# Nine pairs' probabilities transposed as float32r, mean and 1/sigma spread by transposes, PSUM banks taken one by one

## The chip, the core and the metric

One Trainium2 chip, one of its cores. The metric is device time in microseconds (us), from the program's first to its last instruction on that core; lower is better. The kernel before takes 863.33 us (median of 3 runs, 862.97 to 863.5).

## The reference

Causal attention over 4 batches, 12 heads, 448 positions and a head size of 64, in float32, and behind it a layer norm and a feed-forward block with 768 -> 3072 -> 768 and a residual:

```python
scores = scale * np.matmul(q, k.transpose(0, 1, 3, 2))
scores = np.where(mask, -1000000000.0, scores)          # causal
attn = np.exp(scores - np.max(scores, axis=-1, keepdims=True))
attn = attn / (np.sum(attn, axis=-1, keepdims=True) + 1e-09)
x = np.matmul(attn, v)                                  # heads side by side: (4, 448, 768)
xn = (x - mu) / np.sqrt(var + 1e-06) * g_ln
out = x + np.maximum(xn @ w_ch1, 0.0) @ w_ch2
```

## The kernel before

Everything is kept to float32 accuracy. A matmul of float32 operands goes through TensorE in two recorded passes; most matmuls therefore take operands that are split into two float32r parts (high and low, such as wh and wl, xh and xl, kh and kl) and run as three (or two) single-pass float32r matmuls that add up in PSUM.

The work is cut by batch. Two heads make a pair: six pairs for each batch, 24 in all. The 448 positions are cut into four blocks of 112. For a pair, `scores` (or `both`, in batch 0) makes the causal scores in PSUM tiles `sc`; `least` masks, scales and finds the row minimum on VectorE into the SBUF tile `P`; `exps` takes the exponential on ScalarE; `norm` scales P's rows by 1/sum (on GpSimd, VectorE or ScalarE; in the trace `P<-P,r`); `transposes` turns the ten 112x112 blocks of each head with TensorE (`pt<-ident,P`, five groups of four a pair) and moves each group to SBUF as `PT`; `pv` multiplies by the values (`px<-PT,vt`, in batch 0 `px<-PT,rest`) into one PSUM tile in which one head has the upper and the other the lower 64 partitions. Behind the six pairs, `stats` transposes the result for mean and variance (`pln`), `aggr` makes mean and 1/sigma per position, and `spread` (for the last two batches `Pair.banks`) writes them across all 128 partitions (`mb`, `rb`) by multiplying a column, broadcast to 128 columns, with the identity.

The feed-forward block of batches 0 and 1 is `ffn`: 96 steps of 36 matmuls of 448 columns (`ph` into the hidden layer, `po` out of it), with three PSUM banks in rotation (tag `mm`). Weights are converted and split during batch 0 and written to device memory (`keep`, `keep_parts`); later they are read back (`load_full`, six steps ahead; `load_parts`). Batches 2 and 3 are done together by `Pair`, in which seven matmul products take the place of eight (`bX`, `bA`, `bY`, `bZ`); its inputs are made by `inputs` (`xg`, `t` and their parts). The attention of batch 1 runs inside the feed-forward block of batch 0, that of batches 2 and 3 inside that of batch 1 and the end of that of batch 0. So a few transposes, scores or px matmuls always stand between long rows of ph and po.

Nothing is issued as it is written. Each call is recorded as a task in `Plan`; `schedule` gives each task a due time (from its place in the steps of the feed-forward block), and `run` sets the order of all five queues with a list of prices (`cost`): each engine takes the most urgent task that is ready. `together` welds matmuls into one task, so that nothing comes between them. `pick` lets VectorE, ScalarE and GpSimd wait in two cases: where GpSimd or VectorE holds their shared port, and where in the last pass a more urgent task became ready a little later. All DMAs go through SP's queue, in order; a DMA that waits for its data holds up those behind it. `reuse_waits="tile"` pools wait tile by tile; the other pools are closed and opened as a whole (`turn`): `conv` to `late`, `ap` to `pair_x`, and, when the feed-forward block of batch 1 is done, the PSUM pool `ps` to `psb`, whose eight banks `Pair` uses.

All work is issued through one line of `issue` (L513 in the trace), so the rows are told apart by the names of tiles.

Of the kernel before, what the change touches and what calls it, by code (L numbers as in the profile page):

```python
# [28 lines left out]
NF = DFF // P  # L29
HF = NF // 2  # L30
# [14 lines left out]
PASSES, PORT, LEAST, AFTER, URGENT = 6, 300, 150, 1500, 5000  # L45
# [11 lines left out]
KEEP0 = 36  # L57
IDLE = [3, 12]
# [4 lines left out]
ELAG = [2, 5, 7]  # L63
NDVE = 7
# [3 lines left out]
OFF = [C * (i * (i + 1) // 2) for i in range(NC + 1)]  # L68
# [99 lines left out]
class Plan:  # L168
# [99 lines left out]
    def cost(self, t):  # L268
# [189 lines left out]
    def pick(self, e, at, heap, start, port, need, hint, drift):  # L458
# [3 lines left out]
        while heap:  # L462
# [59 lines left out]
def kernel(ctx, tc, qk, v, w1, w2, g, out):  # L522
# [21 lines left out]
    def turn(old, new):  # L544
        def f():
            stacks[old.name].close()
            open_pool(new)

        plan.change(f, [old], [new])

    ident = const.tile([P, P], F32, name="ident")
# [98 lines left out]
    def open_late(_):  # L650
        turn(conv, late[0])
# [43 lines left out]
    class Att:  # L695
# [146 lines left out]

        def transposes(self, p, grp, eng):
# [3 lines left out]
            for h, j in grp:  # L847
# [10 lines left out]
        def pv(self, p):  # L858
# [5 lines left out]
            if self.b == 3:  # L864
                self.xT.append(late[0].tile([P, S], F32, tag="xT", name="xT", bufs=6))
            else:
                self.xT.append(sb.tile([P, S], F32, tag="xT", name="xT", bufs=12))
            for j in range(NC):
                for h in range(2):
                    nc.tensor.matmul(  # L870
                        px[D * h:D * h + D, C * j:], lhsT=vt[:, h, j, :],
                        rhs=self.t.pop(("PT", p, h, j)), start=(j == 0), stop=(j == NC - 1),
                    )
# [26 lines left out]
        def spread(self):  # L900
# [3 lines left out]
            for x in range(NC):  # L904
                nc.tensor.matmul(
                    mb[:, x * C:(x + 1) * C], lhsT=mv[:, x, 0:1].to_broadcast([C, P]),
                    rhs=ident[:C, :C], start=True, stop=True,
# [3 lines left out]
            for x in range(NC):  # L911
                nc.tensor.matmul(
                    rb[:, x * C:(x + 1) * C], lhsT=ve[:, x:x + 1].to_broadcast([C, P]),
                    rhs=ident[:C, :C], start=True, stop=True,
# [39 lines left out]
        def steps(self):  # L954
# [13 lines left out]
            for p, t0 in enumerate(t0s):  # L968
# [81 lines left out]
    class Pair:  # L1050
# [3 lines left out]
        def __init__(self, a, b):  # L1054
            self.at = a, b

# [411 lines left out]
```

## Time and profile before

| | us |
|---|---|
| median of 3 runs (lowest, highest) | 863.33 (862.97, 863.5) |
| the profiled execution, its own time | 865.12 |
| its span, first to last instruction | 863.3 |
| TensorE matmuls busy (share of the span), instructions | 850.3 (98%), 4663 |
| TensorE weight loads busy | 742.7 (86%) |
| VectorE busy | 684.2 (79%) |
| ScalarE busy | 504.4 (58%) |
| GpSimd busy | 268.4 (31%) |

The profile is of one execution. "Busy" is the time in which an engine has at least one instruction under way. Matmuls overlap: each is recorded from its start to a modelled end, so the recorded length of one (0.26 us for a transpose, 0.37 us for 448 columns) is longer than the distance to the next, and it is the distances of starts that tell what one costs. The weight loads (PEld) run ahead of the matmuls. A row of the timeline merges equal instructions in a row: x4 is four of them, and its length is from the first start to the last end.

### The profile page before, as it was taken

What the parts mean: (1) busy time and instruction counts of PE and PEld (TensorE: products, weight loads), DVE (VectorE), ACT (ScalarE), POOL (GpSimd) and SP (SyncE); (2) the same over time, 40 slices, a digit from 0 to 9 for tenths busy, and PEclk for the clock granted to TensorE, in tenths of its full rate; (3) what the DMA queues carried; (4) which work ended last, traced back from release to release, by engine and by line L of the source; (5) the groups of instructions that cost most, each with busy time, mean ns of one, the idle gap of its engine ahead of it and who ended that gap; (6) DMA issues with size and microseconds to landing.
All of it is one profiled execution on the core that took longest, in us unless ns stands there. A gap on an engine that the chain in (4) does not pass through costs nothing.

```text
span 863.3 us, 13819 instructions
## 1 busy us (share of the span) xinstructions
PE 850.3 (98%) x4663; PEld 742.7 (86%) x4663; DVE 684.2 (79%) x1454; ACT 504.4 (58%) x1111; POOL 268.4 (31%) x268
## 2 busy tenths in 40 slices
PE   8999999999999999999999999999999999999997
PEld 5579888888888888888888898989999999999997
DVE  5889888888989986777776579596887778778785
ACT  6898987788887865564454134353544435354450
POOL 4630002210023510010000038454535454464450
PEclk9999999999999999999999999999999999999999
DMA  9665786847669767765554436225243332423424
GB/s 240 222 219 215 307 327 261 320 163 291 249 252 330 261 220 243 257 213 189 186 179 143 160 132 202 93 84 159 63 136 113 93 126 79 127 90 107 123 86 144
DMA packets 59015, 159.77 MB, mean 185 GB/s; under 512 B 6720, under 2 KB 25536, under 8 KB 58944
## 3 DMA queue, kind: packets, MB, share of 16 engines
q1 hardware_dynamic: 58944, 158.89, 54.1%
q8 instruction: 37, 0.61, 0.3%
q14 instruction: 34, 0.28, 0.1%
HBM read 119.15 MB, written 39.71 MB: 184 GB/s over the span
## 4 chain that ended last, share of the span: by engine, by line
PE 89%; DVE 8%; ACT 1%; issue 1%; DMA 1%; POOL 0%; DVEq 0%; ACTq 0%
PE ph L513 21%; PE bX L513 19%; PE po L513 16%; PE bY L513 10%; PE sc L513 6%; PE px L513 6%; PE pt L513 5%; PE bA L513 5%; DVE xg L513 1%; PE pln L513 1%; DVE t L513 1%; DVE qs L513 1%; DVE P L513 1%; DVE xT L513 1%; DVE hx L513 1%
## 5 line engine op out<-in xcount | busy, mean ns | idle before, releaser
L513 ACT ACTIVATE P<-P,nm 112x448 f32<-112x448 f32 (+3 forms) x176 | 91.1, 520 | 39.7 <-DVE nm L513 39.3
L513 POOL TENSOR_TENSOR kl<-qkraw,kh 128x896 fp32r<-128x896 f32 x18 | 40.8, 2266 | 232.4 <-ACT kh L513 104.0
L513 PE MATMUL ph<-xh,wh 128*128 128x448 f32 x288 | 111.4, 388 | 0.1
L513 PE MATMUL po<-hh,wh 128*128 128x448 f32 x288 | 109.3, 383 | 1.9 <-ACT xT2h L513 1.9
L513 PE MATMUL ph<-xl,wh 128*128 128x448 f32 x288 | 105.6, 367 | 0.0
L513 PE MATMUL ph<-xh,wl 128*128 128x448 f32 x288 | 105.5, 366 | 0.0
L513 PE MATMUL po<-hl,wh 128*128 128x448 f32 x288 | 104.2, 367 | 0.0
L513 PE MATMUL po<-hh,wl 128*128 128x448 f32 x288 | 103.3, 367 | 0.0
L513 ACT ACTIVATE wp<-s 128x256 fp32r<-128x256 f32 (+1 forms) x108 | 50.1, 464 | 84.1 <-PE bX L513 35.1
L513 DVE CUSTOM_DVE_ANT_0 P<-sc,mask 112x448 f32<-112x448 f32 (+3 forms) x176 | 73.0, 444 | 26.5 <-PE sc L513 25.9
L513 POOL TENSOR_TENSOR s<-u 128x256 f32<-128x256 f32 (+1 forms) x60 | 56.5, 946 | 93.3 <-DMA u<-scratch 54.3
L513 ACT ACTIVATE wk<-u 128x384 fp32r<-128x384 f32 (+1 forms) x82 | 38.2, 467 | 65.8 <-PE bX L513 47.7
L513 DVE TENSOR_TENSOR wp<-s,wp 128x256 fp32r<-128x256 f32 (+1 forms) x120 | 72.9, 613 | 2.3 <-ACT wp L513 1.9
L513 PEld LDWEIGHTS pt<-ident,P 112*112 112x112 f32 x440 | 48.9, 133 | 15.3 <-ACT PT L513 2.7
L513 PE MATMUL pt<-ident,P 112*112 112x112 f32 x440 | 60.7, 260 | 0.5 <-ACT PT L513 0.4
L513 DVE TENSOR_TENSOR xT<-xT,bX 128x448 f32<-128x448 f32 x72 | 44.5, 618 | 20.8 <-PE bX L513 20.5
L513 POOL TENSOR_TENSOR h<-b,h 128x448 fp32r<-128x448 f32 x36 | 42.2, 1173 | 58.0 <-ACT h L513 31.8
L513 PEld LDWEIGHTS po<-hh,wh 128*128 128x128 f32 x288 | 54.1, 188 | 6.6 <-ACT xT2h L513 2.2
L513 PEld LDWEIGHTS ph<-xh,wl 128*128 128x128 f32 x288 | 54.1, 188 | 4.8
L513 PEld LDWEIGHTS po<-hh,wl 128*128 128x128 f32 x288 | 54.1, 188 | 4.8
L513 PEld LDWEIGHTS ph<-xh,wh 128*128 128x128 f32 x288 | 54.1, 188 | 4.1 <-ACT xh L513 0.4
L513 PEld LDWEIGHTS ph<-xl,wh 128*128 128x128 f32 x288 | 54.5, 189 | 3.3
(163 smaller groups left out, 2165.8 us busy)
## 6 DMA issues: line engine op xcount, KB each, us to landing
raw<-w_dram SPq DMA_DIRECT2D x39, 768.0 KB, 8.1
scratch<-w SPq DMA_DIRECT2D x48, 384.0 KB, 7.0
full<-scratch SPq DMA_DIRECT2D x24, 768.0 KB, 5.4
qkraw<-qk_dram SPq DMA_DIRECT2D x18, 896.0 KB, 5.4
kept<-wl SPq DMA_DIRECT2D x30, 384.0 KB, 6.9
u<-scratch SPq DMA_DIRECT2D x24, 384.0 KB, 3.7
u<-scratch SPq DMA_DIRECT2D x36, 256.0 KB, 2.9
rawx<-w_dram SPq DMA_DIRECT2D x9, 768.0 KB, 10.0
```

What stands on the lines that cost most here:

```text
L513: getattr(getattr(nc, t.engine), method)(*args, **kw)
```

## The change

1. The probabilities of nine pairs (pairs 3 to 5 of batch 2, and all six of batch 3; table `COPIED`) are copied after `norm`, head by head, by a DMA from P into a new tile PR of type float32r (18 DMAs of 112x1120). `transposes` then turns PR with a float32r identity into float32r PSUM. The other fifteen pairs' transposes stay float32. PR lives in a new pool `probs`, two tiles, beside `late`; the pair's `tmp` tiles move to a pool `temps` that opens where `probs` closes.
2. `spread` and `Pair.banks` call `transpose` on the broadcast column where they called `matmul` with the identity: 32 float32 matmuls become 32 float32 transposes.
3. In batch 0, `pv` welds the matmuls of the two heads of a pair (`together`).
4. `Pair` takes its PSUM banks from `ps` one by one, in the order of `BANKS`; the pool `psb` and its turn are gone.
5. The planner: other prices for DMAs and for a float32r transpose; and `pick` holds an engine back only for tasks before its time 70000 (`START`).

```diff
+COPIED = [NP, NP, 3, 0]
+BANKS = [("sc", 2), ("sc", 2), ("pt", 2), ("pt", 2), ("pv", 1), ("mm", 3), ("mm", 3), ("mm", 3)]
-PASSES, PORT, LEAST, AFTER, URGENT = 6, 300, 150, 1500, 5000
+PASSES, PORT, LEAST, AFTER, URGENT, START = 6, 300, 150, 1500, 5000, 70000
...
-            return 60, (x.p[1] - x.p[0]) * n * 4, False
+            rate = 360 if x.p[1] - x.p[0] == P else 240 if x.p[1] - x.p[0] == D else 150 if n == 512 else 330
+            return 60, (x.p[1] - x.p[0]) * n * 4 * 320 / rate, False
...
-                return 0.84 * n, 220, False
+                return 0.84 * n if t.ins[0].dtype == F32 else 56, 220, False
...
-            if shared and port > at + PORT:
+            if shared and port > at + PORT and at < START:
...
-            if hint is not None:
+            if hint is not None and at < START:
...
-    late = [pool("late", 1, reuse_waits="tile")]
+    late = pool("late", 1, reuse_waits="tile")
+    probs = pool("probs", 1, reuse_waits="tile")
+    temps = pool("temps", 1, reuse_waits="tile")
...
-    psb = pool("psb", 8, space=PSUM, reuse_waits="tile")
...
-    ident = const.tile([P, P], F32, name="ident")
+    identr = const.tile([P, P], F32R, name="ident")
+    ident = identr.bitcast(F32)
...
+        def copy(self, p, h):
+
+            t = probs.tile([C, OFF[NC]], F32R, tag="PR", name="PR", bufs=2)
+            nc.sync.dma_start(out=t.bitcast(F32), in_=self.t["P", p, h])
+            self.t["PR", p, h] = t
...
-                    nc.tensor.transpose(pt[:, o:o + C], pp[:, a:a + C], ident[:C, :C])
+                    if ("PR", p, h) in self.t:
+                        pr = self.t["PR", p, h]
+                        nc.tensor.transpose(pt[:, o:o + C].bitcast(F32R), pr[:, a:a + C], identr[:C, :C])
+                    else:
+                        nc.tensor.transpose(pt[:, o:o + C], pp[:, a:a + C], ident[:C, :C])
...
+                if self.b == 0:
+                    nc.together(*calls)
+                    continue
...
             for x in range(NC):
-                nc.tensor.matmul(
-                    mb[:, x * C:(x + 1) * C], lhsT=mv[:, x, 0:1].to_broadcast([C, P]),
-                    rhs=ident[:C, :C], start=True, stop=True,
+                nc.tensor.transpose(
+                    mb[:, x * C:(x + 1) * C], mv[:, x, 0:1].to_broadcast([C, P]), ident[:C, :C]
                 )
...
                     put(pre, t0 + nat[h], self.norm, p, h)
+                    if p >= COPIED[self.b]:
+                        put(pre, t0 + nat[h], self.copy, p, h)
...
         def open_inputs(self):
+            turn(probs, temps)
             turn(ap, pair_x)
...
-                self.bank[b, name] = psb.tile([P, S], F32, tag="b", name="b" + name, bufs=8)
+                tag, bufs = BANKS[self.banked % 8]
+                self.banked += 1
+                self.bank[b, name] = ps.tile([P, S], F32, tag=tag, name="b" + name, bufs=bufs)
...
-        turn(ps, psb)
```

The order of every queue changes. Three places follow, all on TensorE.

The opening, batch 0, where the first pair's px matmuls stand among transposes (pt) and scores (sc); a row with 64x448 is one matmul of one head. Before:

```order
L513 MATMUL pt<-ident,P 112x112 x8
L513 MATMUL px<-PT,rest 64x448
L513 MATMUL pt<-ident,P 112x112 x6
L513 MATMUL px<-PT,rest 64x448
L513 MATMUL px<-PT,rest 64x336 x2
L513 MATMUL px<-PT,rest 64x224 x2
L513 MATMUL px<-PT,rest 64x112 x2
```

Now:

```order
L516 MATMUL pt<-ident,P 112x112 x8
L516 MATMUL sc<-first_qk 112x224 x2
L516 MATMUL pt<-ident,P 112x112 x6
L516 MATMUL px<-PT,rest 64x448 x2
L516 MATMUL px<-PT,rest 64x336 x2
L516 MATMUL px<-PT,rest 64x224 x2
L516 MATMUL px<-PT,rest 64x112 x2
```

The two heads' first px matmuls stood six transposes apart and are now neighbours.

Batch 2, pair 3, the first copied pair: its second and third group of transposes among po matmuls (numbers after a name tell buffers apart; P_3364 and P_3467, later PR_3600 and PR_3680, are its two heads). Before:

```order
L513 MATMUL pt_3685<-ident_82,P_3364 112x112 [waits PE_49]
L513 MATMUL pt_3685<-ident_82,P_3364 112x112 x3
L513 MATMUL po_3584<-hh_1002,wh_3613 128x448
L513 MATMUL po_3584<-hl_1011,wh_3613 128x448
L513 MATMUL po_3584<-hh_1002,wl_3637 128x448
L513 MATMUL pt_3695<-ident_82,P_3364 112x112 [waits DVE_49]
L513 MATMUL pt_3695<-ident_82,P_3364 112x112
L513 MATMUL pt_3695<-ident_82,P_3467 112x112 x2
```

Now:

```order
L516 MATMUL pt_3707<-ident_82,PR_3600 112x112 [waits PE_49]
L516 MATMUL pt_3707<-ident_82,PR_3600 112x112 x3
L516 MATMUL po_3609<-hh_1013,wh_3483 128x448
L516 MATMUL po_3609<-hl_1023,wh_3483 128x448
L516 MATMUL po_3609<-hh_1013,wl_3520 128x448
L516 MATMUL pt_3719<-ident_82,PR_3600 112x112 [waits DVE_49]
L516 MATMUL pt_3719<-ident_82,PR_3600 112x112
L516 MATMUL po_3609<-hh_1013,wh_3483 128x448
L516 MATMUL po_3609<-hl_1023,wh_3483 128x448
L516 MATMUL po_3609<-hh_1013,wl_3520 128x448
L516 MATMUL pt_3719<-ident_82,PR_3680 112x112 [waits DMAHW2_49]
L516 MATMUL pt_3719<-ident_82,PR_3680 112x112
```

The second head's first transposes now wait for a DMA, and three po matmuls have moved ahead of them; from that pair's last scores to this place there are 71 rows in either order.

Near the end of batch 1's feed-forward block, where one po ends and the next begins. Before:

```order
L513 MATMUL po_5795<-hl_1011,wh_5765 128x448
L513 MATMUL po_5795<-hh_1002,wl_5805 128x448
L513 MATMUL po_5795<-hh_1002,wh_5765 128x448
L513 MATMUL po_5939<-hh_1002,wh_5897 128x448 [waits DVE_49,Activation_49]
L513 MATMUL po_5795<-hl_1011,wh_5765 128x448
L513 MATMUL po_5795<-hh_1002,wl_5805 128x448
L513 MATMUL po_5939<-hl_1011,wh_5897 128x448
L513 MATMUL po_5949<-hh_1002,wh_5800 128x448
```

Now:

```order
L516 MATMUL po_5903<-hh_1013,wh_5808 128x448
L516 MATMUL po_5903<-hl_1023,wh_5808 128x448
L516 MATMUL po_5903<-hh_1013,wl_5847 128x448
L516 MATMUL po_5979<-hh_1013,wh_5842 128x448 [waits DVE_49]
L516 MATMUL po_5979<-hl_1023,wh_5842 128x448
L516 MATMUL po_5979<-hh_1013,wl_5813 128x448 [waits DMAHW4_49]
```

Three banks of po were open at once (5795, 5939, 5949); now each po is finished before the next begins.

## Rows read from the trace of the kernel before

**Rows 1.** Windows: us, busy time of each engine (instructions), granted clock, DMA share, GB/s

```profile
67.00:300.00 233.00, 232.54 (x1337) 203.66 (x1336) 208.13 (x433) 191.27 (x377) 45.12 (x26) 1.00 0.73 272
300.00:505.00 205.00, 205.00 (x1214) 177.13 (x1213) 145.65 (x357) 99.33 (x244) 19.20 (x11) 1.00 0.60 200
...
550.00:859.00 309.00, 308.23 (x1509) 281.89 (x1507) 241.47 (x429) 138.56 (x304) 144.65 (x148) 1.00 0.35 110
```

**Rows 2.** The same view of two stretches of the opening (PE, PEld, DVE, ACT, POOL)

```profile
34.00:52.00 18.00, 18.00 (x128) 11.69 (x125) 14.29 (x57) 17.00 (x47) 12.29 (x24) 1.00 0.34 104
52.00:65.00 13.00, 11.96 (x79) 9.16 (x77) 12.77 (x37) 12.07 (x29) 3.13 (x2) 1.00 0.68 238
```

**Rows 3.** Timeline of TensorE: start us, us, engine, line, operation, tile, shape, count

```profile
112.60 0.55 PE L513 MATMUL pt<-ident,P 112*112 112x112 f32 x4
112.92 0.45 PE L513 MATMUL ph<-xh,wh 128*128 128x448 f32 x1
113.21 0.37 PE L513 MATMUL ph<-xl,wh 128*128 128x448 f32 x1
```

**Rows 4.** Groups of weight loads: form, count | busy us, mean ns | idle before us

```profile
L513 PEld LDWEIGHTS pt<-ident,P 112*112 112x112 f32 x440 | 48.9, 133 | 15.3 <-ACT PT L513 2.7 <-POOL P L513 2.1 <-DVE nm L513 1.4
...
L513 PEld LDWEIGHTS sc<-kl,qs 128*112 128x112 f32 x144 | 25.2, 175 | 2.4
```

**Rows 5.** Timeline of the weight loads of one group of scores

```profile
102.63 0.17 PEld L513 LDWEIGHTS sc<-kl,qs 128*112 128x112 f32 x1
102.72 0.18 PEld L513 LDWEIGHTS sc<-kh,qs 128*112 128x112 f32 x1
```

**Rows 6.** Timeline of the matmuls of the same group

```profile
102.63 0.21 PE L513 MATMUL sc<-kh,qs 128*112 128x112 f32 x1
102.68 0.26 PE L513 MATMUL sc<-kl,qs 128*112 128x112 f32 x1
```

**Rows 7.** Timeline of TensorE at batch 1's spread: its start and the stream behind it

```profile
264.75 1.04 PE L513 MATMUL mb<-ident,mv 112*128 112x112 f32 x8
...
266.74 0.36 PE L513 MATMUL po<-hl,wh 128*128 128x448 f32 x1
```

**Rows 8.** Timeline of TensorE in the opening: a split pair, and a whole one

```profile
15.88 0.96 PE L513 MATMUL px<-PT,rest 112*64 112x448 f32 x2
...
17.49 2.10 PE L513 MATMUL px<-PT,rest 112*64 112x448 f32 x14
19.52 0.79 PE L513 MATMUL pt<-ident,P 112*112 112x112 f32 x6
...
46.83 2.23 PE L513 MATMUL px<-PT,rest 112*64 112x448 f32 x16
```

**Rows 9.** Timeline of VectorE in the opening: a conversion of 128x896

```profile
24.90 0.91 DVE L513 CAST kh<-qkraw 128x896 fp32r<-128x896 f32 x1
```

**Rows 10.** Timeline of VectorE at the pair's inputs

```profile
531.24 1.55 DVE L513 TENSOR_TENSOR t<-xg,t 128x448 f32<-128x448 f32 x1
532.71 0.61 DVE L513 TENSOR_TENSOR xT<-po,xT 128x448 f32<-128x448 f32 x1
```

**Rows 11.** Timeline of TensorE there: in brackets the idle time before, and its releaser

```profile
533.47 0.45 PE L513 MATMUL po<-hh,wh 128*128 128x448 f32 x1 [1.87 <-ACT xT2h L513]
```

**Rows 12.** Timelines of ScalarE and VectorE: the last scalings of two heads

```profile
301.32 1.40 ACT L513 ACTIVATE P<-P,r 112x336 f32<-112x336 f32 x3
...
334.31 0.95 DVE L513 TENSOR_SCALAR P<-P,r 112x112 f32<-112x112 f32 x3
```

**Rows 13.** Timeline of TensorE: the groups that hold these heads' first transposes

```profile
306.59 0.55 PE L513 MATMUL pt<-ident,P 112*112 112x112 f32 x4
...
341.57 0.55 PE L513 MATMUL pt<-ident,P 112*112 112x112 f32 x4
```

**Rows 14.** DMA issues from 280 to 460 us: count, KB each, median us to landing

```profile
kept<-wl SPq DMA_DIRECT2D x20, 384.0 KB, 6.7
kept<-wl SPq DMA_DIRECT2D x9, 192.0 KB, 3.5
```

More of the change, by code (lines that the diff above doesn't have):

```diff
@@ L29 @@
 NF = DFF // P
+OFF = [C * (i * (i + 1) // 2) for i in range(NC + 1)]
 HF = NF // 2
@@ L539, with turn @@
     ap = pool("ap", 1, side="right")
-    late = [pool("late", 1, reuse_waits="tile")]
+    late = pool("late", 1, reuse_waits="tile")
+    probs = pool("probs", 1, reuse_waits="tile")
+    temps = pool("temps", 1, reuse_waits="tile")
     pair_x = pool("pair_x", 1, side="right", reuse_waits="tile")
-    psb = pool("psb", 8, space=PSUM, reuse_waits="tile")
-    def turn(old, new):
+    def turn(old, *new):
         def f():
             stacks[old.name].close()
-            open_pool(new)
-        plan.change(f, [old], [new])
-    ident = const.tile([P, P], F32, name="ident")
+            for x in new:
+                open_pool(x)
+        plan.change(f, [old], new)
+    identr = const.tile([P, P], F32R, name="ident")
+    ident = identr.bitcast(F32)
     mask = ap.tile([C, S], BF16, name="mask")
@@ L650, in open_late @@
     def open_late(_):
-        turn(conv, late[0])
+        turn(conv, late, probs)
     def weights_ahead(start):
@@ L864, in pv @@
             if self.b == 3:
-                self.xT.append(late[0].tile([P, S], F32, tag="xT", name="xT", bufs=6))
+                self.xT.append(late.tile([P, S], F32, tag="xT", name="xT", bufs=6))
             else:
@@ L868, in pv @@
             for j in range(NC):
-                for h in range(2):
-                    nc.tensor.matmul(
-                        px[D * h:D * h + D, C * j:], lhsT=vt[:, h, j, :],
-                        rhs=self.t.pop(("PT", p, h, j)), start=(j == 0), stop=(j == NC - 1),
-                    )
+                calls = [
+                    ("matmul", (px[D * h:D * h + D, C * j:],), dict(
+                        lhsT=vt[:, h, j, :], rhs=self.t.pop(("PT", p, h, j)), start=(j == 0), stop=(j == NC - 1),
+                    ))
+                    for h in range(2)
+                ]
+                if self.b == 0:
+                    nc.together(*calls)
+                    continue
+                for method, args, kw in calls:
+                    nc.tensor.matmul(*args, **kw)
             move(self.xT[p], px)
@@ L911, in spread @@
             for x in range(NC):
-                nc.tensor.matmul(
-                    rb[:, x * C:(x + 1) * C], lhsT=ve[:, x:x + 1].to_broadcast([C, P]),
-                    rhs=ident[:C, :C], start=True, stop=True,
+                nc.tensor.transpose(
+                    rb[:, x * C:(x + 1) * C], ve[:, x:x + 1].to_broadcast([C, P]), ident[:C, :C]
                 )
@@ L1062, in banks @@
                     for x in range(NC):
-                        nc.tensor.matmul(
-                            dst[:, x * C:(x + 1) * C], lhsT=col(x).to_broadcast([C, P]),
-                            rhs=ident[:C, :C], start=True, stop=True,
+                        nc.tensor.transpose(
+                            dst[:, x * C:(x + 1) * C], col(x).to_broadcast([C, P]), ident[:C, :C]
                         )
@@ L1082, in tmp @@
         def tmp(self, name):
-            return late[0].tile([P, S], F32, tag="tmp", name=name, bufs=NTMP)
+            return temps.tile([P, S], F32, tag="tmp", name=name, bufs=NTMP)
         def parts(self, src, hi, lo, eng):
@@ L1374 @@
         nc.gpsimd.affine_select(
-            out=ident, in_=ident, compare_op=ALU.not_equal, fill=1.0, base=0, pattern=[[-1, P]], channel_multiplier=1,
+            out=identr, in_=ident, compare_op=ALU.not_equal, fill=1.0, base=0, pattern=[[-1, P]], channel_multiplier=1,
         )
```

3 lines of the change are left out of this document (1 added, 2 removed).

## Prediction

> **What bounds the kernel now.** I read the stretches first. From 300 to 505 us TensorE is busy for all 205.00 us, VectorE for 145.65 and ScalarE for 99.33; from 550 to 859 us it issues 1509 matmuls in 309.00 us, which is 0.2048 us for each, and is idle for 0.8 [rows 1]. The granted clock is 1.00 in both rows, the 2.4 GHz level. So after the opening, TensorE's queue is the path: a nanosecond taken out of it there comes off the end, as long as nothing else becomes late. The opening (to about 67 us, where the dense stream of ph matmuls starts) is different: from 34 to 52 us TensorE counts as busy throughout while ScalarE is busy 17.00 of 18.00 us, and from 52 to 65 us VectorE is busy 12.77 of 13.00 [rows 2]. There three engines share the bound, and a gain of one is worth a part of itself.
>
> **Transposes of nine pairs as float32r.** Today four transposes stand in a stream of 448-column matmuls. From the start of the first to the start of the second matmul behind them is 113.21 - 112.60 = 0.61 us; less one matmul of 0.205 the four cost 0.406 [rows 3]. The four last (0.55 us from first start to last end, less the 0.26 that one of 112 columns is recorded with [rows 6]) start 0.095 apart, so 0.38 of it is their own pace and 0.026 the change from one kind to the other. What sets 0.095? Two things can: 112 columns streamed as float32, or 112 columns of weights loaded. A float32r stream of 112 columns is shown by the scores: the matmul after it starts at 102.68, 0.05 later [rows 6]. The loads are shown too: consecutive float32r loads of 112 columns start 0.09 apart (102.63, 102.72) [rows 5] and each is recorded with 175 ns [rows 4], that is some 80 to 85 ns more than its pace. A load for a transpose, of the same 112 columns, is recorded with 133 ns [rows 4]; less the same it would keep a pace of 48 to 53. So the float32 stream is today's limit, and with a float32r stream of 0.050 the load is about as long. No row shows a float32r transpose; between 0.050 (stream alone) and 0.096 (loads at the pace of the scores') I take 0.054, the upper end for a load of the short kind, since a transpose's load is of that kind already. Four then cost 4 x 0.054 + 0.026 = 0.242, a gain of 0.164. Nine pairs have five groups each: 45 x 0.164 = **7.4 us**, bounds 0 and 8.1.
>
> The Trainium skill ("TensorE: Matmul & The Clock Gate", section "LDWEIGHTS (loading the stationary operand)") gives the load as the number of columns over 1.2 per ns, whatever the data: 93 ns for 112 columns. By that rule the transposes are load-bound already and float32r gains nothing. The 0.09 us between loads of the scores agrees with it; the 133 ns recorded for a transpose's load against 175 for the same columns speaks against it.
>
> **Mean and 1/sigma by transposes.** Each spread is now eight matmuls in float32, which the trace counts as two passes each: sixteen from 264.75 until the stream is back at 266.74, less one 0.205, is 1.79 us, or 0.112 a pass [rows 7]. Eight transposes at 0.095 + 0.03 cost 0.79. There are three such spreads inside the dense stream (batch 1, and two for the pair): 3 x 1.0 = 3.0. In the opening the second half of batch 0's spread stands in front of the ph stream, 0.5 more; its first half is ready before VectorE asks. **3.5 us**, bounds 2.7 (a transpose no faster than a pass) and 4.0.
>
> **The opening.** Batch 0's probabilities times values run the two heads in two halves of the array, and side by side only if they are adjacent in the queue. Pair 0 today: 0.96 us for one head's first matmul alone, then 2.10 for the rest; a pair kept whole takes 2.23. Each has 0.07 of tail under what follows (17.49 + 2.10 = 19.59, and the next starts at 19.52), so it is 0.89 + 2.03 = 2.92 against 2.16 [rows 8]. The order shows five of six pairs split, so TensorE loses at least 5 x 0.76 = 3.8 us, and the change welds all six. But VectorE has 0.2 us of idle left from 52 to 65 us and ScalarE 1.0 from 34 to 52 [rows 2]: what TensorE finishes earlier they must also finish earlier. VectorE's idle of 3.7 us from 34 to 52 is what can be closed. I take **2.0 us**; upper bound 3.8; lower bound -0.9, because the order hands VectorE one more conversion of 128x896 ahead of the first ph, 0.91 us by its like [rows 9], and ScalarE one less.
>
> **The wait at 531 us.** TensorE stands for 1.87 us and resumes at 533.47 [rows 11]. VectorE, busy with the pair's inputs, had taken 1.55 us over one subtraction from 531.24 and only then got to the addition that empties a bank of po, from 532.71 to 533.32 [rows 10]; the first matmul of the next po waits for VectorE and ScalarE, whose own work hung on the same subtraction. Before, two po were interleaved there and ended together; in the new order they come one after the other, with some 36 matmuls (7.4 us) between the end of one and the next need of a bank. Gain **1.9**, bounds 0 and 2.3 (with the 0.46 us of idle before 300 us).
>
> **The copies.** Each of the 18 heads gets a DMA of 112x1120 float32 (490 KB) between its last scaling and its first transpose. That interval is cover only in its present length: in the order the first transpose stands as many rows behind the scores as before. The shortest, for the first copied pair: last scaling ends 301.32 + 1.40 = 302.72, and its first transpose is the third of the four from 306.59, at 306.78: 4.06 us. The pair's other head has 4.2; of the other sixteen the shortest is 334.31 + 0.95 = 335.26 to 341.57, 6.31 us [rows 12, 13], the longest 10.4, the mean 7.9. The nearest DMAs of that stretch land after 6.7 us (384 KB) and 3.5 us (192 KB) [rows 14]; both go to device memory, a copy stays on chip. I take 4.6 us: the first two heads are late by about 0.5 each, **-1.0 us**; bounds 0 (under 4 us) and -5.9 (6.7 us: 2.6 + 2.5 + 0.4 + 0.3 + 0.1). Behind a copy that waits for its scaling stand the next kept store, qkraw load and weight load (full) in SP's queue. Nobody waits soon for a kept store; the code issues full six steps ahead and qkraw four, and a step lasts 5 us (96 of them in the 482 us from 67 to 549). That cover hides a wait of a few us, and I cost it at nothing; were it gone, a late qkraw would cost TensorE the excess, which the next term's bound takes in.
>
> **Banks one by one; no look-ahead after 70 us.** None of TensorE's waits in the trace stands at the change from po to bX, where the whole PSUM pool is turned over today; so taking the banks one by one gains 0 there. The planner no longer holds VectorE, ScalarE and GpSimd back for a coming urgent task or for the shared port after its time 70000, so every order changes. TensorE's idle from 67 to 549 us is 0.46 up to 300 us, nothing to 505 [rows 1], and the 1.87 at 531, 2.3 in all; a new order can bring as much again. I take **-0.8**, bounds 0 and -2.3.
>
> Sum: 7.4 + 3.5 + 2.0 + 1.9 - 1.0 - 0.8 = **13.0 us**. The profiled execution took 865.12 us (span 863.3), so 852.1 for one like it; the median of the runs, 863.33, is 1.8 lower, and the forecast on it is **850.3 us**.
>
> **Rivals.**
> 1. Loads bind: float32r transposes keep 0.096. For it: the pace of the scores' loads [rows 5]. Against: 133 ns against 175 [rows 4]. The first term falls away: 850.3 + 7.4 = 857.7 us. By the rule of the Trainium skill above, this is what happens.
> 2. Copies land somewhat late, at 6.7 us as the kept stores do: 5.9 instead of 1.0, 855.2 us; together with other small waits up to 861.
> 3. Slower: the copies land after 9 us or more, because the DMA engines are already busy 0.60 of the time from 300 to 505 us [rows 1] and the copies add to that. Then every head waits: 4.9 + 4.8 for the first pair and 20.8 over the other sixteen (what each interval lacks of 9 us, added up), some 30 us against 14 gained: 879 us. It decides from a landing of about 7.8 us, where the sum of the waits reaches the 14. Against it: both rows of that stretch [rows 14] lie below.
> 4. The float32r matmuls do not run where they should, or new waits eat all: no change.
>
> **How the numbers follow.** Forecast (845 to 855): 0.70. Rival 1 (855 to 860): 0.15. Rival 2: 0.07. Rival 3: 0.05. Rival 4: 0.03. All best bounds give 863.3 - (8.1 + 4.0 + 3.8 + 2.3) = 845.1; the range reaches up over rival 1: 845 to 858. A measurement here tells 0.2% (1.7 us) from no change: faster 0.92, same 0.03, slower 0.05.
>
> **What would show it.** Groups of four float32r transposes in the stream costing 0.24 us instead of 0.41, and their loads still at 133 ns; spreads of eight instructions in 0.8 us; the first dense ph some 2 us earlier than 66.8; no wait at the pair's inputs; waits of TensorE on the copy for the first copied pair alone. The prediction is wrong if the transposes stay 0.095 apart, if waits on the copy come back pair after pair, or if the opening ends later than today.

## The result, and the profile after

The changed kernel takes 854.6 us (median of four) against 863.18 for the kernel before: a ratio of 0.9895, interval 0.9876 to 0.9915. In a second comparison (after_again) it took 853.83 us (853.42 to 854.09) against 864.59, ratio 0.9874, 0.986 to 0.9889. One of the first four executions, the profiled one, was disturbed (1366.73 us, at a mean granted clock of 0.656; the other three took 853.36 to 855.4) and isn't in the ratio, so every line of after below is from the second comparison's run of the same kernel, with a span of 851.9 us against 863.3.

The path is still TensorE's queue. The first view is that of the windows: stretch, busy time and instructions of PE, PEld, DVE, ACT and POOL, granted clock, DMA share, GB/s. The last window is moved by 10 us, since the pair starts at 538.95 instead of 549.19:

```profile
34.00:52.00 18.00, 15.71 (x112) 11.25 (x109) 15.30 (x47) 15.43 (x38) 11.55 (x17) 0.91 0.41 140
52.00:65.00 13.00, 10.86 (x71) 7.83 (x71) 12.63 (x35) 12.27 (x28) 3.48 (x2) 1.00 0.66 233
...
67.00:300.00 233.00, 233.00 (x1339) 203.31 (x1338) 210.48 (x432) 192.48 (x380) 45.48 (x26) 1.00 0.77 287
300.00:505.00 205.00, 205.00 (x1225) 177.59 (x1224) 153.46 (x368) 96.40 (x233) 23.97 (x15) 1.00 0.69 230
540.00:848.00 308.00, 308.00 (x1508) 281.51 (x1506) 243.43 (x432) 135.41 (x299) 144.09 (x148) 1.00 0.36 111
```

Against [rows 1], the 0.46 us of idle before 300 us is gone, and there are 11 more matmuls in the 205 us from 300 to 505. In the opening TensorE is no longer busy throughout from 34 to 52 us: 15.71 of 18.00, where [rows 2] has 18.00; and its granted clock is 0.91 there, where it was 1.00.

A group of four transposes of a copied pair, in the timeline of TensorE [rows 3]; its weight loads in their own timeline; and then all such loads from 300 to 505 us [rows 4] (count | busy us, mean ns | idle us):

```profile
363.05 0.43 PE L516 MATMUL pt<-ident,PR 112*112 112x112 f32 x4
363.32 0.45 PE L516 MATMUL ph<-xh,wh 128*128 128x448 f32 x1
363.60 0.36 PE L516 MATMUL ph<-xl,wh 128*128 128x448 f32 x1
```

```profile
362.88 0.46 PEld L516 LDWEIGHTS pt<-ident,PR 112*112 112x112 f32 x4
363.29 0.19 PEld L516 LDWEIGHTS ph<-xh,wh 128*128 128x128 f32 x1
```

```profile
L516 PEld LDWEIGHTS pt<-ident,PR 112*112 112x112 f32 x176 | 18.7, 133 | 3.9
```

From the group's start to the second matmul behind it is 0.55; less one matmul of 0.205 the four cost 0.345, where 0.406 was and 0.242 was forecast. The median of the 39 groups that stand in a clean stream is 0.342. The loads are recorded with 133 ns, as forecast. The starts of the matmuls alone would not have told it: within a group they stand 0.057 apart (median), close to the forecast's 0.054. But of the loads, the first of which runs ahead (362.88), the last starts at 363.21 (362.88 + 0.46 less 0.13) and the next one, for the ph behind, 0.08 later, and the ph starts 0.03 after its load.

A pair of px in the opening [rows 8], whole now, and batch 1's spread [rows 7], TensorE's timeline:

```profile
16.70 2.11 PE L516 MATMUL px<-PT,rest 112*64 112x448 f32 x16
...
262.94 0.55 PE L516 MATMUL mb<-ident,mv 112*128 112x112 f32 x4
263.33 0.55 PE L516 MATMUL rb<-ident,ve 112*128 112x112 f32 x4
263.64 0.46 PE L516 MATMUL po<-hh,wh 128*128 128x448 f32 x1
263.94 0.36 PE L516 MATMUL po<-hl,wh 128*128 128x448 f32 x1
```

The 16 matmuls of the pair are recorded with 2.11 in all. Eight transposes of the spread cost 263.94 - 262.94 - 0.205 = 0.79. The same reckoning gives 0.40 for the half spread in the opening (0.89 before) and 1.55 for the pair's two (3.58 before, as two of [rows 7]).

What TensorE waits for from 67 to 540 us, by groups, two of them shown (count | busy us, mean ns | idle us before):

```profile
L516 PE MATMUL pt<-ident,P 112*112 112x112 f32 x175 | 24.2, 259 | 0.0
L516 PE MATMUL pt<-ident,PR 112*112 112x112 f32 x180 | 19.4, 230 | 0.0
```

No group there has any idle time: the 1.87 us of [rows 11] are gone, and the copies are never waited for. In the DMA issues from 280 to 460 us [rows 14] the copies land sooner than the kept stores of 384 KB (count, KB each, median us to landing):

```profile
PR<-P SPq DMA_DIRECT2D x17, 490.0 KB, 4.1
kept<-wl SPq DMA_DIRECT2D x19, 384.0 KB, 6.2
kept<-wl SPq DMA_DIRECT2D x10, 192.0 KB, 3.9
```

**Where the 11.4 us between the two spans went.** Four landmarks divide a span: the start of the dense ph stream (the first ph with xl), the first bX of the pair, the last matmul, the end.

| stretch | before | after | gain |
|---|---|---|---|
| opening, to the dense stream | 66.56 | 65.11 | 1.45 |
| dense stream to the pair | 482.63 | 473.84 | 8.79 |
| the pair | 309.02 | 309.02 | 0.00 |
| last matmul to the end | 5.06 | 3.94 | 1.12 |

The middle's 8.79 are 2.6 for the float32r transposes (from the run pr_f32, below), 3.0 for the three spreads, 2.3 for the two waits that are gone, and 0.5 for five transposes that now stand ahead of the dense stream (125 instead of 120); 0.3 stays over. The last line wasn't forecast: with the end of before unchanged, the run b_weld below has 4.1 there too, so it most likely belongs to the one execution profiled of before, which is a long one (865.12 us, median 863.33), rather than to the change.

### The profile page after: what moved, and what is told of

Same layout as the page of the kernel before. It is cut to its first block, busy times and chain, and to the rows that moved or that the text cites. A ratio compares the mean times of both kernels' runs of the same rounds, so it can differ in the third digit from the quotient of the medians.

```text
span 1364.9 us, 13747 instructions
## 1 busy us (share of the span) xinstructions
PE 1355.3 (99%) x4631; PEld 882.4 (65%) x4631; DVE 696.4 (51%) x1466; ACT 508.4 (37%) x1099; POOL 265.2 (19%) x268
## 4 chain that ended last, share of the span: by engine, by line
PE 99%; DVE 0%; DMA 0%; issue 0%
PE ph L516 21%; PE po L516 21%; PE bX L516 21%; PE bY L516 11%; PE px L516 6%; PE sc L516 6%; PE bA L516 5%; PE pt L516 5%; PE pln L516 1%; PE idle L516 0%; DMA first_qk<-qk_dram 0%; PE mb L516 0%; PE rb L516 0%; DVE w L516 0%; DVE xT L516 0%; DVE stat L516 0%
## 5 line engine op out<-in xcount | busy, mean ns | idle before, releaser
L516 PE MATMUL ph<-xh,wh 128*128 128x448 f32 x288 | 157.7, 548 | 0.0
L516 PE MATMUL po<-hh,wh 128*128 128x448 f32 x288 | 155.3, 539 | 0.0
L516 PE MATMUL po<-hl,wh 128*128 128x448 f32 x288 | 152.2, 528 | 0.0
L516 PE MATMUL po<-hh,wl 128*128 128x448 f32 x288 | 152.1, 528 | 0.0
L516 PE MATMUL ph<-xl,wh 128*128 128x448 f32 x288 | 151.6, 526 | 0.0
L516 PE MATMUL ph<-xh,wl 128*128 128x448 f32 x288 | 151.5, 526 | 0.0
L516 ACT ACTIVATE wk<-u 128x256 fp32r<-128x256 f32 (+1 forms) x78 | 35.8, 461 | 156.1 <-PE bX L516 111.8
L516 PEld LDWEIGHTS ph<-xh,wh 128*128 128x128 f32 x288 | 64.3, 223 | 24.3 <-issue 9.0
L516 PEld LDWEIGHTS po<-hl,wh 128*128 128x128 f32 x288 | 64.4, 223 | 24.0 <-issue 8.5
L516 PE MATMUL bY<-h,wp 128*128 128x448 f32 x216 | 79.7, 529 | 0.0
L516 PE MATMUL bX<-h,wk 128*128 128x448 f32 x216 | 78.2, 528 | 0.0
```

The lines of the kernel that those rows point to most:

```text
L516: getattr(getattr(nc, t.engine), method)(*args, **kw)
```

## The experiments

Medians are of 4 to 11 runs, and each ratio is to runs of before on the same chip (medians 864.59 for the first five rows, 863.55 to 864.61 for the rest); load80 and stream80 ran once. "Stream" is where the dense stream starts, "idle" is TensorE's idle time from there to the pair, both in the profiled execution. load80 and stream80 leave out a part of the output.

| run | median us | ratio, interval | stream | idle | stream to pair | pair |
|---|---|---|---|---|---|---|
| before | 864.59 | 1 | 66.56 | 2.3 | 482.63 | 309.02 |
| after_again | 853.83 | 0.9874, 0.986 to 0.9889 | 65.11 | 0 | 473.84 | 309.02 |
| pr_f32 | 856.02 | 0.99, 0.9886 to 0.9915 | 64.66 | 0 | 476.48 | 308.96 |
| no_copy | 856.99 | 0.9911, 0.9897 to 0.9926 | 65.08 | 0 | 476.52 | 309.12 |
| no_weld | 857.0 | 0.9912, 0.9895 to 0.9928 | 68.01 | 0 | 474.06 | 309.26 |
| turned | 854.55 | 0.9898, 0.9885 to 0.9912 | 64.31 | 0.1 | 474.37 | 309.30 |
| load80 | 851.97 | | 65.48 | 0 | 471.75 | 308.98 |
| stream80 | 850.6 | | 64.26 | 0.2 | 471.39 | 309.10 |
| b_weld | 862.16 | 0.9986, 0.9974 to 0.9998 | 61.22 | 4.6 | 484.93 | 308.96 |
| old_prices | 857.27 | 0.9916, 0.99 to 0.9931 | 66.13 | 0 | 475.07 | 310.30 |
| hold | 863.41 | 0.9988, 0.9977 to 1.0 | 65.45 | 6.9 | 483.31 | 309.82 |
| turned_hold | 863.68 | 0.9994, 0.9985 to 1.0004 | 64.39 | 6.9 | 483.46 | 309.00 |
| cheap_copy | 858.71 | 0.9919, 0.9889 to 0.9949 | 63.40 | 7.0 | 482.30 | 309.28 |

**The changed kernel again**, as it stands.

> The changed kernel as it stands, for a profile at the full clock. Measured so far about 854 us, 4 us above the forecast of 850.3. Theory A (the transposes are mis-sized): groups of four float32r transposes cost 0.33 us or more in the stream instead of the forecast 0.24, and everything else is as forecast. Theory B (the opening gives nothing): groups at 0.24, but the dense ph stream starts no earlier than about 66.8 us. Theory C (waits on the copies): groups at 0.24, the opening 2 us shorter, and TensorE idle for 3 to 5 us in front of transposes of PR.

The lines above are its lines. Of the theories A fits: 0.345 for a group, with the stream 1.5 us earlier and no wait for PR.

**What paces a float32r transpose.** First the transposes of the copied pairs in float32 again, with the planner's price left as it was, so that TensorE's order stays:

```
-  nc.tensor.transpose(pt[:, o:o + C].bitcast(F32R), pr[:, a:a + C], identr[:C, :C])
+  nc.tensor.transpose(pt[:, o:o + C], pr[:, a:a + C].bitcast(F32), ident[:C, :C])
```

> The changed kernel with its copies, and the same order on TensorE, but the 180 transposes of copied probabilities read PR as float32 with the float32 identity. If float32r transposes keep a pace of 0.054 us, this is 7.4 us slower than the changed kernel, about 861.5. If loads bind (0.095 for either type), the same, about 854. If theory A holds, in between: about 3.5 us slower.

A group of pr_f32 in TensorE's timeline:

```profile
368.19 0.55 PE L516 MATMUL pt<-ident,PR 112*112 112x112 f32 x4
368.51 0.45 PE L516 MATMUL ph<-xl,wh 128*128 128x448 f32 x1
368.80 0.37 PE L516 MATMUL ph<-xh,wl 128*128 128x448 f32 x1
```

0.61 - 0.205 = 0.405, as in the kernel before; the stretch from the stream to the pair is 2.64 us longer than after, and the median 2.2. So the float32r transposes are worth 2.2 to 2.6 us, not 7.4. Their loads start 0.078 apart (median), where those of float32 transposes start 0.095 to 0.099 apart. Whether that 0.078 is the load or the stream of the identity, two runs tell, each with one of the two sizes cut to 80 (other lines of the edits left out):

```
-  nc.tensor.transpose(pt[:, o:o + C].bitcast(F32R), pr[:, a:a + C], identr[:C, :C])
+  nc.tensor.transpose(pt[:80, o:o + C].bitcast(F32R), pr[:, a:a + 80], identr[:C, :C])    (load80)
+  nc.tensor.transpose(pt[:, o:o + k].bitcast(F32R), pr[:k, a:a + C], identr[:k, :k])      (stream80, k = 80 but for the first block)
```

> The changed kernel, in which the float32r transposes of the copied pairs take 80 instead of 112 columns of probabilities as weights (the last 32 keys of each block are left out of the output), with 112 moving columns of the identity as before. If the load of the weights paces these transposes, their loads come 0.056 us apart instead of 0.078 (80/112 of it), and a group of four in the stream costs about 0.25 us instead of 0.34. If the moving columns pace them, or a fixed cost for each instruction, a group stays at 0.34.

> The changed kernel, in which the float32r transposes of the copied pairs' second to fourth key blocks take 80 instead of 112 moving columns (the last 32 queries of each block are left out for these keys), with 112 columns of weights as before. If the moving columns pace these transposes, they come 0.056 us apart and a group of four such costs about 0.25 us instead of 0.34. If the load of the weights paces them, or a fixed cost for each instruction, it stays at 0.34.

TensorE's timeline of load80, then its weight loads there, and all of them from 300 to 505 us:

```profile
362.64 0.38 PE L516 MATMUL pt<-ident,PR 112*80 112x112 f32 x4
362.86 0.44 PE L516 MATMUL ph<-xh,wh 128*128 128x448 f32 x1
363.14 0.37 PE L516 MATMUL ph<-xl,wh 128*128 128x448 f32 x1
```

```profile
362.48 0.41 PEld L516 LDWEIGHTS pt<-ident,PR 112*80 112x80 f32 x4
362.83 0.19 PEld L516 LDWEIGHTS ph<-xh,wh 128*128 128x128 f32 x1
```

```profile
L516 PEld LDWEIGHTS pt<-ident,PR 112*80 112x80 f32 x176 | 16.0, 118 | 4.5
```

TensorE's timeline of stream80, and all its loads:

```profile
406.20 0.41 PE L516 MATMUL pt<-ident,PR 80*112 80x80 f32 x4
406.44 0.47 PE L516 MATMUL po<-hh,wh 128*128 128x448 f32 x1
406.75 0.37 PE L516 MATMUL po<-hl,wh 128*128 128x448 f32 x1
```

```profile
L516 PEld LDWEIGHTS pt<-ident,PR 80*112 80x112 f32 x108 | 11.6, 133 | 2.8 <-DMA PR<-P 0.3
```

With 80 columns of weights a group costs 0.50 - 0.205 = 0.295 (median of 39: 0.299) and the loads start 0.063 apart; with 80 streamed columns it costs 0.345 (median of 24: 0.342) and they stay at 0.078. So the loads pace the float32r transposes, and the identity's stream doesn't. The expectation of load80 was a little off in size: the pace doesn't shrink by 80/112 but by 15 ns, as the recorded length does (133 to 118). In both, the pace is the recorded length less 55. The two cuts aren't quite pure: load80 also writes 80 instead of 112 partitions of the output, and stream80 also reads 80 instead of 112 partitions of the probabilities; neither was tried apart. That stream80's stretch is 2.45 us shorter than after's isn't the transposes: its px matmuls stream fewer columns too, and the 16 of a copied pair take 1.79 instead of 2.11.

**The copies alone.** No pair is copied, all transposes read P in float32:

```
-COPIED = [NP, NP, 3, 0]
+COPIED = [NP, NP, NP, NP]
-        turn(conv, late, probs)
+        turn(conv, late, temps)
...
-            turn(probs, temps)
```

> The changed kernel without the 18 copies: all transposes read P as float32. The forecast's own terms: 7.4 us of gain lost and 1.0 us of waits on the copies saved, so 6.4 slower, about 860.5. If the copies cost TensorE 3 to 5 us (theory C), only 2.5 to 4.5 us slower, 856.5 to 858.5.

Against pr_f32, which copies and gains nothing by it, the stretch from the stream to the pair is the same (476.52 and 476.48), and the intervals overlap: the 18 copies cost nothing that these runs show, in DMA traffic or in waits. The time, 3.2 us above the changed kernel's, lies where the expectation put waits on the copies; the reason is another, that the float32r transposes are worth 2.6 and not 7.4.

**The weld.** First taken out of the changed kernel, then put alone into the kernel before:

```
-                if self.b == 0:
+                if self.b == 9:      (no_weld)
```

> The changed kernel with batch 0's pv matmuls of the two heads recorded one by one, as before. The forecast: 2.0 us slower, about 856. If ScalarE and VectorE set the end of the opening (theory B), no difference (within 0.5). If TensorE alone does, 3.8 us slower, about 858.

> The kernel before with one part of the change alone: batch 0's probabilities times values are kept in pairs of heads. Taking the weld out of the changed kernel cost 2.9 us in the opening. Theory 1, the weld is worth as much wherever it stands: the dense stream of ph starts 2.9 us earlier than 66.6 us and the time is 0.9966 of before. Theory 2, what TensorE finishes earlier is taken back in the order of before by VectorE and ScalarE: the stream starts 0 to 1.5 us earlier, ratio 0.998 to 1.0.

Without it the changed kernel's stream starts at 68.01 instead of 64.3 to 65.5 (the eight profiles of kernels with one and the same order up to there), and the time is 3.2 us longer. Put alone into the kernel before, for which the planner then makes an order of its own (VectorE's differs from 14 us on), it brings the stream 5.3 us forward, more than either theory allowed; but 2.3 us of that come back as new waits, and the time is 0.9986 of before. By the medians it is 1.4 us and not the 3.0 that are left: the profiled execution of before is a long one, so 5.3 is the upper end. What TensorE waits for from 16 to 62 us (us in total, times, longest us), in b_weld:

```profile
PE pln L513 <- DVE stat L513: 1.7, 3, 0.9
```

and in the changed kernel:

```profile
PE pt L516 <- DVE PT L516: 1.6, 1, 1.6
PE pt L516 <- DVE stat L516: 1.2, 1, 1.2
PE pln L516 <- DVE stat L516: 1.0, 3, 0.4
PE pln L516 <- DVE xT L516: 0.5, 1, 0.5
```

So the weld is worth 3 to 5 us in the opening, each time with the order that the planner makes for it, and against b_weld's order the changed kernel's gives most of it back: 4.3 us of waits on VectorE against 1.7, and five more transposes (0.5 us) ahead of the stream. That is 3.1 us; the two starts, 61.22 and 65.11, differ by 3.9, although the changed kernel saves 0.5 at its spread. That leaves 1.3 us.

A part of them is TensorE's clock. After the wait of 1.6 us, which ends at 41.80, the granted clock falls in after_again; in pr_f32, with the same order and the same wait, it stays up. The windows of after_again and of pr_f32:

```profile
43.00:46.00 3.00, 3.00 (x16) 2.30 (x16) 2.23 (x8) 2.27 (x4) 3.00 (x5) 0.56 0.42 133
43.00:46.00 3.00, 3.00 (x25) 2.25 (x25) 2.61 (x8) 2.17 (x4) 3.00 (x5) 1.00 0.09 37
```

The eight profiles fall into two kinds by it. In four the clock falls in the opening, behind this wait (after_again, no_copy) or behind the one of 1.2 us at 60 us (load80, hold), and the stream starts at 65.1 to 65.5; in the other four it stays up, and the stream starts at 64.3 to 64.7. By the middle of the second kind, 64.4, the clock is worth some 0.7 of after_again's 65.11, and 0.6 of the 1.3 stay open.

What makes the wait of 1.2 us can be seen too. The statistics that TensorE waits for stand on VectorE behind a scaling of 112x4, which ends together with a subtraction on GpSimd. VectorE's timeline and GpSimd's in after_again:

```profile
59.50 1.38 DVE L516 TENSOR_SCALAR r<-sm 112x4 f32<-112x4 f32 x1
58.41 2.45 POOL L516 TENSOR_TENSOR kl<-qkraw,kh 128x896 fp32r<-128x896 f32 x1 [12.02 <-ACT kh L516]
```

The same scaling took 0.15 us at 53.48, with nothing on GpSimd. b_weld has such a meeting too (1.07 us), so this isn't what sets the two orders apart.

**What makes that order.** The change also gives the planner new prices for its DMAs, which change when it thinks the opening's inputs arrive. With the old price for all, and with the old price for all but the copies, which get a tenth:

```
-  rate = 360 if x.p[1] - x.p[0] == P else 240 if x.p[1] - x.p[0] == D else 150 if n == 512 else 330
+  rate = 320                                                                    (old_prices)
+  rate = 320 if (t.outs + t.ins)[0].buf.name != "PR" else 3200                  (cheap_copy)
```

> The changed kernel with the planner's old price for a DMA (320 bytes a ns for every shape). In the order of before the weld alone brought the dense stream of ph 5.3 us forward (66.56 to 61.22); in the changed kernel it starts at 64.3 to 65.5 in six profiles, although mean and 1/sigma cost less there. Theory 1: the new prices set an order of the opening that gives back 3 to 4 us of the weld; with the old ones the stream starts at 60.5 to 62 and the time is 850 to 852. Theory 2: the prices cost the opening nothing, and something else (the transposes, the copies) changes its order: stream at 64 to 65.5, 853.8.

> The changed kernel with the planner's old price for every DMA but the copies of the probabilities, which get a tenth of it. The plan then orders the opening as in the kernel before with the weld alone (word for word on TensorE and VectorE up to the first ph), where the dense stream started at 61.2 us. Theory 1: the 3 to 4 us that the changed kernel's opening lacks lie in its order alone: the stream starts at 60.5 to 61.5 us, TensorE has at most 2 us of waits in the opening, and the time is 849.5 to 851. Theory 2: what the opening gains comes back as waits behind it, as with the weld alone in the old order (3.5 us from 100 to 300 us), or a copy is now used too early: 852 to 855.

Theory 1 of old_prices fell: the plan took a third order, whose stream starts at 66.13 (with a granted clock of 0.50 from 61 to 64 us), and the kernel is 3.4 us slower than the changed one: 1.0 in the opening, 1.2 up to the pair, 1.3 in the pair. In cheap_copy the opening has the order of b_weld (VectorE's is the same up to 69 us), and up to VectorE's first xg it was 3 us ahead of after (58.82 against 62.05, and 57.81 in b_weld). Then twelve matmuls that only keep TensorE busy meanwhile (idle) took 1.6 us longer, with a granted clock of 0.54 from 58 to 61 us. TensorE's timeline in cheap_copy:

```profile
58.17 4.25 PE L516 MATMUL idle<-wh 128*128 128x448 f32 x12
```

and in b_weld:

```profile
57.39 2.68 PE L513 MATMUL idle<-wh 128*128 128x448 f32 x12
```

Behind the opening, cheap_copy lost more than that. What TensorE waits for from 60 us on:

```profile
PE pt L516 <- DVE stat L516: 2.7, 1, 2.7
PE pt L516 <- DMA PR<-P: 2.2, 2, 1.1
PE pln L516 <- ACT xT L516: 1.3, 1, 1.3
PE ph L516 <- DVE wl L516: 0.8, 1, 0.8
```

That is theory 2's mechanism: the order's gain came back, 2.2 us of it as waits for copies. They land after 4.1 us as before; the plan, told that they are quick, left two of them too little cover. Its size was missed: 852 to 855 was expected, the median is 858.71, and the six times range from 853.26 to 862.13; the profiled one, 860.73, is among the long ones. What spreads them stays open. No run that does the whole work has a lower median than the changed kernel.

**The wait at the pair's inputs, and the planner's look-ahead.** The prediction put the wait's end down to po groups that are no longer interleaved. In the order, po tiles alternate 24 times in the changed kernel; in the traces, two po matmuls in a row have the same operands' names (two po side by side) 32 times in the kernel before, and never in the changed one. The pair's own PSUM pool and its turn bring the interleaving back:

```
+    psb = pool("psb", 8, space=PSUM, reuse_waits="tile")
...
-                self.bank[b, name] = ps.tile([P, S], F32, tag=tag, name="b" + name, bufs=bufs)
+                self.bank[b, name] = psb.tile([P, S], F32, tag="b", name="b" + name, bufs=8)
...
+        turn(ps, psb)
```

> The changed kernel with the pair's eight banks in a pool of their own again, so that the whole PSUM pool is turned over where the pair starts, as before. Theory 1, the prediction's: taking the banks one by one gains 0, and the wait of 1.87 us at 531 us went because the planner's new order no longer interleaves po groups: the time stays at 853.8 us, and there is no wait at the pair's inputs. Theory 2: the turn is what made the planner interleave the po groups (in the order, po tiles alternate 126 times with the turn and 24 times without), so the wait comes back with it: TensorE stands for about 1.9 us at the pair's inputs and the time is 855.4 to 856.2 us.

po alternates 126 times now (34 such neighbours in the trace), and no wait came back; the intervals of the two ratios just overlap. So the bank change is what ended the interleaving, but the interleaving alone doesn't make the wait. Then the look-ahead, in force to the end, with the turn and without:

```
-PASSES, PORT, LEAST, AFTER, URGENT, START = 6, 300, 150, 1500, 5000, 70000
+PASSES, PORT, LEAST, AFTER, URGENT, START = 6, 300, 150, 1500, 5000, 1 << 30
```

> The changed kernel with the pair's own PSUM pool and its turn again, and with the planner's look-ahead for urgent tasks and for the shared port in force to the end. With the turn alone the po groups were interleaved again, but no wait came back. Theory 1: the look-ahead made the order with the wait near the pair's inputs, so with both the wait of 1 to 2 us comes back and the time is 855 to 856. Theory 2: neither rule makes the wait; it is an accident of that one order and is not there: 854 to 854.6.

> The changed kernel with the planner's look-ahead in force to the end instead of to its time 70000. The opening has the same order on TensorE, VectorE and ScalarE. The prediction's step: dropping the look-ahead costs 0.8 us of new waits, bounds 0 and 2.3, so this is up to 2.3 us faster, 853 by its middle value. Rival: TensorE has no wait after 67 us in the changed kernel, so nothing is to be had: 853.8, or up to 2 us slower with a wait that the look-ahead makes.

Both expectations missed by far. The wait at the pair's inputs isn't in turned_hold either, so what made it in the kernel before stays open. With the look-ahead kept, all the rest of the change is worth 0.6 us by the medians in hold and 0.4 in turned_hold, and with the interval up to 2. The opening and the pair are within 0.8 us of the changed kernel's; the loss is in between, and it is waits of TensorE. In hold, from 67 us on:

```profile
PE pln L516 <- DVE xT L516: 3.2, 2, 2.7
PE pt L516 <- ACT PT L516: 2.3, 2, 2.0
PE pt L516 <- DVE PT L516: 1.4, 1, 1.4
```

The longest, at 158 us, can be followed on three engines. VectorE's timeline in hold:

```profile
152.25 3.06 DVE L516 TENSOR_SCALAR P<-P,r 112x112 f32<-112x112 f32 x4
...
157.57 0.62 DVE L516 COPY xT<-px 128x448 f32<-128x448 f32 x1
```

GpSimd's:

```profile
152.41 2.09 POOL L516 TENSOR_TENSOR kl<-qkraw,kh 128x896 fp32r<-128x896 f32 x1 [0.85 <-ACT kh L516]
```

and TensorE's, in brackets what it stood for:

```profile
158.24 0.32 PE L516 MATMUL pln<-ident,xT 128*112 128x128 f32 x1 [2.69 <-DVE xT L516]
...
159.24 0.58 PE L516 MATMUL po<-hh,wl 128*128 128x448 f32 x1
159.62 0.58 PE L516 MATMUL po<-hh,wh 128*128 128x448 f32 x1
```

In the changed kernel the same four scalings are over before GpSimd starts on kl (151.43), and the move of px is given to ScalarE. VectorE's timeline and ScalarE's there:

```profile
149.63 1.19 DVE L516 TENSOR_SCALAR P<-P,r 112x112 f32<-112x112 f32 x4
```

```profile
153.82 0.53 ACT L516 ACTIVATE xT<-px 128x448 f32<-128x448 f32 x1
```

In hold the four scalings run beside kl and take 3.06 us instead of 1.19; the reductions, exponentials and the move of px queue up behind them, and TensorE gets xT 2.69 us late. Then its clock falls too: from 158.87 on the matmuls start 0.37 to 0.38 apart instead of 0.205, eight of them, 1.4 us more. The windows of hold show it as a granted clock of 0.79 from 160 to 165 us. Waits of 6.9 and 1.4 for the clock are 8.3 of the 9.5 us by which hold's middle is longer. What is shown is that the plan with the look-ahead has these waits and the plan without has none (turned_hold has the same ones as hold, the longest 2.75 us); that this very rule put the scalings beside kl is an argument only.

## Why the prediction was right, and where it was not

The forecast was 850.3 us in a range of 845 to 858. The time lies in the range, on the slow side of the likeliest case, and by the forecast's own sum (13.0 us) some 2 to 4 us are lacking: the medians of the two comparisons differ by 8.6 and 10.8. The range confirms little of the working: it reaches up over rival 1, so that even pr_f32, with no float32r transpose at all, lies in it with 856.02. The largest term came out at a third of its size, and the time came near all the same in part because the look-ahead and the copies, costed at 1.8 together, cost nothing; that is luck. By its steps:

- **Float32r transposes, 7.4: measured 2.2 to 2.6.** The step that failed is the pace of a load, 48 to 53 ns, got by taking from the recorded 133 ns the 80 to 85 that the scores' loads (175) are longer than their pace. The excess isn't the same for every load: the runs show 55 for these, hence 78 ns. The load is the bound, as rival 1 said, but at 0.078 and not at the scores' 0.09. With it the prediction's own formula gives 4 x 0.078 + 0.026 = 0.338 a group, measured 0.342. The Trainium skill ("TensorE: Matmul & The Clock Gate", section "LDWEIGHTS (loading the stationary operand)") gives a load as its columns over 1.2 per ns, by which an estimate is 93 ns for 112 columns and 67 for 80; the runs show 78 and 63. By its rule the load binds, which the float32r transposes bear out; its figure is too slow for them, so that it left no gain at all.
- **Spreads by transposes, 3.5: right.** 1.0 for batch 1, 2.0 for the pair, 0.5 in the opening.
- **The opening, 2.0: right in size, by two errors.** After the spread's 0.5 and the moved transposes, the profile shows 1.5 (1.1 to 2.3 by the eight starts). But the weld, with the order that came with it in b_weld, brings up to 5.3, above the bound of 3.8 that counted TensorE's split pairs alone, and the changed kernel's order takes 3 to 4 back: 2.6 more of waits on VectorE, 0.5 of transposes and some 0.7 of TensorE's clock. The prediction read from the idle times how much could be gained and priced the new order at one conversion; that the order itself could cost TensorE 4.3 us of waits it didn't see.
- **The wait at 531 us, 1.9: gone, but not for the reason given.** The interleaving of po can be there without the wait (turned).
- **Banks one by one, 0: right** as far as the runs tell: 0.7 us between the medians of turned and after_again, which ran on different chips, and 2 us between their ratios, whose intervals just overlap. It does change the order.
- **The look-ahead, -0.8: the sign was wrong.** Together with the wait at 531 us, it was priced at 1.9 - 0.8 = 1.1; measured are 2.3, since no wait at all is left after 67 us. Its full weight shows only beside the rest: with the look-ahead in force, the shortened queue of TensorE runs into waits of 6.9 us and the change gains half a microsecond. The parts don't add up.
- **The copies, -1.0: 0.** The estimate of 4.6 us for a landing was near (4.1); the wait of 0.5 on each of the first two heads didn't come.

Put together: 2.6 + 3.5 + 1.5 + 2.3 = 9.9, and the 1.1 at the end of the one execution of before, which the forecast hadn't, makes 11.0 of the 11.4 us between the spans.

Of the rivals, the second and third (late copies) would have shown waits for PR, and there are none; cheap_copy shows what they look like when the cover is gone. The second half of the fourth, new waits that eat all, is what hold and turned_hold show: 0.9988 and 0.9994.

## What to carry to other kernels

Take the pace of an instruction from the distance between starts in a run of the same kind, and of the part that binds: here the starts of the loads told it, and those of the matmuls didn't. A recorded length less a constant from another kind gives a wrong one. Where a planner sets the order, count a rule or a price that is changed with it as a part of its own, and try the change without it: here, in the one order that was made with it, the rule decided whether 10 us of shorter work arrived at the end or came back as waits. And a copy made ahead cost nothing here as long as the plan knew how long it takes.

## What the runs showed of the hardware

- A weight load for a float32r transpose of 112 partitions keeps a pace of 78 ns for 112 columns and 63 for 80, recorded with 133 and 118; float32 transposes of 112 streamed columns keep 95 to 99.
- Four scalings on VectorE took 3.06 us beside a GpSimd subtraction of 128x896 (hold), and 1.19 without it; one scaling of 112x4 took 1.38 beside such a subtraction and 0.15 without it (after_again).
- After a wait of 2.69 us TensorE's granted clock fell to its 1.2 GHz level for some 3 us (matmuls of 448 columns 0.38 apart instead of 0.205); after waits of 1.97 us and 1.42 us in the same run, after the 1.87 of [rows 11], and after one of 2.68 us in cheap_copy the matmuls behind show no such fall. In the opening it falls in some executions and not in others of the same order: behind a wait of 1.6 us in two of eight (0.56 from 43 to 46 us in after_again), behind one of 1.2 in two others (0.50 from 60 to 62 us in hold, where the twelve idle matmuls took 3.54 us, and 2.68 to 2.72 in after_again, turned, no_copy and pr_f32). What decides is left open; it is most of why the starts of one order differ by 1.2 us.
- Copies of 490 KB from one on-chip buffer to another landed after 4.1 us, sooner than stores of 384 KB (6.2 us).
